# Scores in the four quarters of the array, and token group 0's product operands made during batch 1's attention

## The chip, the cores and the metric

The kernel runs on one core of one Trainium2 chip. The metric is the device time of one execution in microseconds (us). The engines are named as in the profile: PE is TensorE's matmul side, PEld its weight loads, DVE VectorE, ACT ScalarE, POOL GpSimd, SP the engine that issues the DMAs.

## The reference, cut to what matters

Attention with a window of 128 keys over 2 batches, 8 heads, 576 tokens of head size 64; its output (1152 tokens of 512) goes through 4 experts that are all used, then through a gated layer.

```python
scores = scale * q @ k.T                      # per batch and head, 576x576, head size 64
mask = (rel >= 0) & (rel < 128)               # rel = query position - key position
scores = where(mask, scores - slope[h] * abs(rel), -1e9)
attn = exp(scores - max); attn = attn / (sum(attn) + 1e-9)
x = (attn @ v) as 1152x512
for e in range(4):                            # w1: 512x1024, w2: 1024x512
    out += p[:, e] * (relu(x @ w1[e]) @ w2[e])
xn = out / rms(out) * g                       # then silu(xn @ w_gate) * (xn @ w_val) @ w_out
```

## The kernel before

**Attention.** Work goes by pairs of heads: 2 batches x 4 pairs, called pair 0 to 7 here. The 576 queries of a pair are nine tiles `t` of 64, and both heads stand in one tile: `qS` comes from the host filled up with zeros, so that its 128 rows hold head A's 64 dimensions and head B's, and its 128 columns head A's 64 queries (zeros in B's rows) and head B's. One 128x128 matmul (L311) of up to 192 key columns gives a tile's scores of both heads. Two tiles share a PSUM buffer `s`, and there are two such buffers. DVE adds the bias and takes the row's extreme (L312, the rows call it CUSTOM_DVE_ANT_0, the listings of order ISA), ACT takes the exponential with its sum (L316), POOL multiplies by the reciprocal (L326). The results stand in a score buffer `tt`, of which there are two, for pairs taken by turns. `values` then transposes them on PE (`pst`, L348), ACT and DVE copy these out as `pt` and `pe` (L333, L335), and PE multiplies by v: `po` and, for the last query tile, `pp` (L354), 64 output columns a head, the two heads in the two column halves of the array. ACT and DVE write the result as a high and a low part, `xh` and `xl` (L371, L372). `values` of a pair is emitted after the scores of the pair behind it. The order on each engine inside this part is that of the emitting code as the tile framework schedules it.

**Fillers.** Batch 0 is token group 0, batch 1 group 1. Unit 0, the first half of expert 0, needs no sums: `hidden` (`psa`, L207) for group 0 runs as a filler of the attention of batch 1, then `mixed` (`psb`, L221, four token tiles) after it.

**Behind the attention** the code is laid out by `Plan`: each engine's order is fixed by hand-set costs (Plan.START, RATE) and due times. First unit 0's `hidden` for group 1 (8 groups of 12 matmuls, L207), then its `out_plain` for token tiles 4 to 8 (L782). Units 1 to 7 use a product scheme with 7 products instead of 8 (`products`, L678, of 6 matmuls each, 42 a call); a unit makes four such calls: weight halves 0 and 1 for group 0, then both for group 1. It needs three token operands as they are and four made from sums: `token_sums` (for each group 14 DVE operations of 576 columns and 4 on ACT; `stage`, `th`, `tl`), and sums of the weights (`load_unit`, `raw` and `wb`). For unit 1 all of that, for both groups, is planned on DVE and ACT behind the attention. DVE also splits `wa`, `op` and folds PSUM results into `y` (L810, L812). On each engine the instructions stand in that order, so one that waits holds up those behind it.

Token operand 4 overwrites a quarter of group 0's own `xh`, `xl`; it can only be made when the fillers have read that.

Of the kernel before, what the change touches and what calls it, by code (L numbers as in the profile page):

```python
# [11 lines left out]
F32 = mybir.dt.float32  # L12
# [4 lines left out]
ALU = mybir.AluOpType  # L17
# [129 lines left out]
def tile_fused(ctx: ExitStack, tc: tile.TileContext, qS, kS, vS, probs, w1, w2, wgv, wo, g, out):  # L147
# [93 lines left out]
    y = ypool.tile([P, NTT, DM], F32, tag="y", name="y")  # L241


    h = hpool.tile([P, 4, NT], F32, tag="h", name="h")
    with (
# [15 lines left out]
        rel = rl_p.tile([P, WIN], F32, name="rel")  # L261
        bias = rl_p.tile([P, H // 2, WIN], F32, name="bias")
        for r in range(2):
# [14 lines left out]
        def load_pair(b, p):  # L278
            qt = qk_p.tile([P, NQ, P], F32, tag="q", name="qt")
            kt = qk_p.tile([P, S], F32, tag="k", name="kt")  # L280
            nc.sync.dma_start(out=kt, in_=kS[b, p])
            for t0, t1 in ((0, 3), (3, NQ)) if (b, p) == (0, 0) else ((0, NQ),):
                state["dma"] = nc.sync.dma_start(out=qt[:, t0:t1, :], in_=qS[b, p, :, t0:t1, :])
            if p % 2 == 0:
                vt = v_p.tile([P, 5, 4 * D], F32, tag="v", name="vt")
                hs = slice(p * P, p * P + 4 * D)
                nc.sync.dma_start(out=vt[:, :4, :], in_=vS[b, : 4 * P, hs].rearrange("(k p) d -> p k d", p=P))
                nc.sync.dma_start(out=vt[:D, 4, :], in_=vS[b, 4 * P :, hs])
                state["vt"] = vt
            if b == 0:  # L290
                for r in range(2):
                    rows = slice(r * D, (r + 1) * D)
                    nc.vector.tensor_scalar(
                        out=bias[rows, p, :], in0=rel[rows], scalar1=-8.0 * 2.0 ** (-8.0 * (2 * p + r + 1) / H), scalar2=None,
                        op0=ALU.mult,
                    )
            return qt, kt, state["vt"]

        def scores(n, p, qt, kt):
            tt = tts[n % 2]  # L300
            st = st_p.tile([P, 4, NQ], F32, tag="st", name="st")
            spans = []
            for t in range(NQ):
                k0 = max(0, t - 2) * D
                nk = (t + 1) * D - k0
                if t % 2 == 0 or t == NQ - 1:
                    s = ps_s.tile([P, 2, 4 * D], F32, tag="s", name="s")
                sp = s[:, t % 2, :nk]
                c0 = WIN - nk + (D if t % 2 else 0)
                spans.append(tt[:, t, c0 : c0 + nk])  # L310
                nc.tensor.matmul(sp, lhsT=qt[:, t, :], rhs=kt[:, k0 : k0 + nk], start=True, stop=True)  # L311
                nc.vector.tensor_tensor_reduce(  # L312
                    out=spans[t], in0=sp, in1=bias[:, p, WIN - nk :], scale=-0.125, scalar=3.0e38,
                    op0=ALU.add, op1=ALU.min, accum_out=st[:, 0, t : t + 1],
# [22 lines left out]
        def values(b, p, tt, vt):  # L337
            pt = pt_p.tile([P, 4, 4, P], F32, tag="pt", name="pt")
            pe = pt_p.tile([D, P], F32, tag="pe", name="pe")
            po = ps_o.tile([P, 4 * P], F32, tag="po", name="po")  # L340
            pp = ps_p.tile([P, D], F32, tag="pp", name="pp")
            for kb in range(5):
# [14 lines left out]

                for j in range(2):
                    r = slice(j * D, (j + 1) * D)
                    if kb < 4:  # L360
                        m = min(n, 4 if kb < 3 else 2)
                        mm(j, po[r, kb * P : kb * P + m * D], pt[:, kb, :m, r], kb == 0, kb == 3)
                for j in range(2):
                    r = slice(j * D, (j + 1) * D)
                    if kb == 3:
                        mm(j, pp[r, :], pt[:, 3, 2, r], True, False)
                    if kb == 4:
                        mm(j, pp[r, :], pe[:, r], False, True)
            for ps, w, o in ((po, 4 * P, 0), (pp, D, 4 * P)):
# [4 lines left out]
        def filler():  # L374
# [12 lines left out]
            for t in range(4):  # L387
                yield lambda t=t: mixed(t)

        state = {}  # L390
        order = [(b, p) for b in range(B) for p in range(H // 2)]
        ready, queue = [], []
        todo = filler()
        for n in range(len(order) + 1):
# [24 lines left out]


# [3 lines left out]
    tpool = ctx.enter_context(tc.tile_pool(name="tpool", bufs=1))  # L424
    HT = S // 2
    th = [xh] + [tpool.tile([P, 2, S], F32R, name=f"th{i}") for i in range(3)]
    tl = [xl] + [tpool.tile([P, 2, S], F32R, name=f"tl{i}") for i in range(3)]
    pl = Plan()
# [48 lines left out]
    class Stage:  # L477
# [6 lines left out]
        def first(self, engines, n, needs, emit, due):  # L484
            def emit_first(e):
                self.tile = tmp.tile([P, 512 if self.tag == "s" else S], F32, tag=self.tag, name="stage", bufs=RINGS[self.tag])
                emit(e)

            return pl.later(engines, n, needs, emit_first, due, (rings[self.tag], self.done))
# [3 lines left out]


    def second(n, gr):

        a, b = slice(gr * S, gr * S + HT), slice(gr * S + HT, (gr + 1) * S)
        k, tok = {0: (0, a), 1: (2, a), 2: (2, b), 4: (0, b)}.get(n, (0, slice(gr * HT, (gr + 1) * HT)))
        i = {3: 3, 5: 1, 6: 2}.get(n, 0)
        return [x[:, k : k + 2, tok] for x in (th[i], tl[i])]  # L500

    def operand(hi, lo, end):
        return (lambda k: hi[:, k, :]), (lambda k: lo[:, k, :]), end
# [555 lines left out]
```

## Time and profile before

| | |
|---|---|
| time, median of 3 runs | 696.7 us (696.02 to 697.32) |
| profiled execution: its time / its span | 696.54 / 694.8 us |
| busy in the span | PE 98%, PEld 88%, DVE 64%, ACT 42%, POOL 7% |
| attention (first scores to the last `psa`) | 4.8 to 82.8 us |
| unit 0's `psb` | 85.35 to 96.09 us |
| unit 0 for group 1, `hidden` and `out_plain` | 96.09 to 122.25 us |
| unit 1's four calls of `products` start at | 122.25, 128.13, 142.86, 148.44 us |

A busy PE is a matmul in flight, not PE at its peak. Stretches, waits and the chain are read by time, since the bound is not the same in each.

### The profile page before, as it was taken

What the parts mean: (1) busy time and instruction counts of PE and PEld (TensorE: products, weight loads), DVE (VectorE), ACT (ScalarE), POOL (GpSimd) and SP (SyncE); (2) the same over time, 40 slices, a digit from 0 to 9 for tenths busy, and PEclk for the clock granted to TensorE, in tenths of its full rate; (3) what the DMA queues carried; (4) which work ended last, traced back from release to release, by engine and by line L of the source; (5) the groups of instructions that cost most, each with busy time, mean ns of one, the idle gap of its engine ahead of it and who ended that gap; (6) DMA issues with size and microseconds to landing.
All of it is one profiled execution on the core that took longest, in us unless ns stands there. A gap on an engine that the chain in (4) does not pass through costs nothing.

```text
span 694.8 us, 10177 instructions
## 1 busy us (share of the span) xinstructions
PE 681.3 (98%) x3928; PEld 610.4 (88%) x3928; DVE 445.9 (64%) x946; ACT 295.0 (42%) x666; POOL 47.8 (7%) x100
## 2 busy tenths in 40 slices
PE   8999999699999999999999999999999999999997
PEld 6777798698998988989989989889998999899986
DVE  5765558868477585584784865887887775831233
ACT  5876533354262352442533524754546534411210
POOL 5852310000000000000000000000000000000000
PEclk9999999799999999999999999999999999999999
DMA  8650001112103002012030030103434441200012
GB/s 284 227 191 28 1 1 32 31 60 63 59 2 121 1 31 92 1 32 90 1 92 31 19 103 16 62 0 122 152 122 145 136 144 62 91 1 1 1 45 92
DMA packets 16304, 48.38 MB, mean 70 GB/s; under 512 B 1792, under 2 KB 4224, under 8 KB 16256
## 3 DMA queue, kind: packets, MB, share of 16 engines
q1 hardware_dynamic: 16256, 47.74, 20.8%
q8 instruction: 31, 0.51, 0.3%
q14 instruction: 17, 0.14, 0.1%
HBM read 45.37 MB, written 2.36 MB: 69 GB/s over the span
## 4 chain that ended last, share of the span: by engine, by line
PE 93%; DVE 4%; DMA 1%; ACT 1%; issue 0%; SPq 0%; POOL 0%; DVEq 0%
PE ps_b L782 11%; PE ps_d L782 9%; PE ps_a L782 9%; PE ps_c L782 8%; PE ps_c L678 7%; PE ps_b L207 6%; PE ps_d L678 6%; PE ps_c L207 6%; PE ps_d L207 5%; PE ps_a L207 5%; PE ps_a L678 5%; PE ps_b L678 4%; PE s L311 3%; PE po L354 3%; PE pst L348 2%; PE psa L207 2%
## 5 line engine op out<-in xcount | busy, mean ns | idle before, releaser
L782 PE MATMUL ps_b<-wa,op 128*128 128x512 f32 x348 | 82.2, 390 | 0.0
L782 PEld LDWEIGHTS ps_b<-wa,op 128*128 128x128 f32 x348 | 64.8, 188 | 13.0
L447 ACT ACTIVATE op<-h 128x512 fp32r<-128x512 f32 x95 | 56.5, 621 | 35.2 <-PE ps_d L782 11.9
L782 PE MATMUL ps_d<-wa,op 128*128 128x512 f32 x288 | 67.8, 390 | 0.0
L440 DVE TENSOR_TENSOR op<-h,op 128x512 fp32r<-128x512 f32 x95 | 63.0, 684 | 6.3 <-ACT op L447 6.0
L782 PEld LDWEIGHTS ps_d<-wa,op 128*128 128x128 f32 x288 | 54.0, 188 | 11.1
L782 PE MATMUL ps_a<-wa,op 128*128 128x512 f32 x264 | 61.8, 389 | 0.0
L782 PEld LDWEIGHTS ps_a<-wa,op 128*128 128x128 f32 x264 | 49.5, 188 | 10.2
L782 PE MATMUL ps_c<-wa,op 128*128 128x512 f32 x240 | 56.2, 389 | 0.0
L782 PEld LDWEIGHTS ps_c<-wa,op 128*128 128x128 f32 x240 | 45.1, 188 | 9.3
L207 PE MATMUL ps_b<-xh,wb 128*128 128x384 f32 x160 | 42.4, 335 | 0.0
L447 ACT ACTIVATE wb<-raw 128x512 fp32r<-128x512 f32 (+1 forms) x63 | 30.6, 526 | 22.6 <-DVE raw L440 22.6
L207 PE MATMUL ps_a<-xh,wb 128*128 128x384 f32 x144 | 38.3, 336 | 0.7 <-ACT xh L447 0.7
L739 ACT ACTIVATE h<-r 128x576 f32<-128x576 f32 x28 | 19.2, 686 | 46.6 <-DVE r L443 46.6
L207 PE MATMUL ps_c<-xh,wb 128*128 128x384 f32 x144 | 38.0, 334 | 0.0
L316 ACT ACTIVATE tt<-tt,st 128x192 f32<-128x192 f32 (+2 forms) x72 | 30.8, 429 | 11.0 <-DVE st L312 10.5
L440 DVE TENSOR_TENSOR wb<-raw,wb 128x512 fp32r<-128x512 f32 (+1 forms) x63 | 34.0, 567 | 0.5
L207 PE MATMUL ps_d<-xh,wb 128*128 128x384 f32 x128 | 33.9, 334 | 0.0
L608 ACT ACTIVATE stage<-raw 128x512 f32<-128x512 f32 x36 | 23.9, 666 | 21.8 <-DMA raw<-in_wo 12.1
L311 PE MATMUL s<-kt,qt 128*128 128x192 f32 (+1 forms) x144 | 31.7, 333 | 1.2 <-DMA qt<-in_qS 0.8
L312 DVE CUSTOM_DVE_ANT_0 tt<-s,bias 128x192 f32<-128x192 f32 (+2 forms) x72 | 23.3, 331 | 12.7 <-PE s L311 9.3
L326 POOL TENSOR_SCALAR tt<-tt,st 128x192 f32<-128x192 f32 (+2 forms) x72 | 27.9, 408 | 31.7 <-DVE st L324 15.7
(200 smaller groups left out, 1535.7 us busy)
## 6 DMA issues: line engine op xcount, KB each, us to landing
raw<-in_w SPq DMA_DIRECT2D x32, 512.0 KB, 3.6
raw<-in_wgv SPq DMA_DIRECT2D x24, 512.0 KB, 3.7
raw<-in_wo SPq DMA_DIRECT2D x12, 512.0 KB, 3.5
qt<-in_qS SPq DMA_DIRECT2D x7, 576.0 KB, 5.3
kt<-in_kS SPq DMA_DIRECT2D x8, 288.0 KB, 3.2
out_y<-acc SPq DMA_DIRECT2D x9, 256.0 KB, 2.0
vt<-in_vS SPq DMA_DIRECT2D x4, 512.0 KB, 5.1
qt<-in_qS SPq DMA_DIRECT2D x1, 384.0 KB, 4.5
```

Of the source, the lines that this page charges most:

```text
L207: nc.tensor.matmul(ps, lhsT=a, rhs=x[:, k, tok], start=(n == 0), stop=(n == 3 * KC - 1))
L311: nc.tensor.matmul(sp, lhsT=qt[:, t, :], rhs=kt[:, k0 : k0 + nk], start=True, stop=True)
L312: nc.vector.tensor_tensor_reduce(out=spans[t], in0=sp, in1=bias[:, p, WIN - nk :], scale=-0.125, scalar=3.0e38, op0=ALU.add, op1=ALU.min, ...
L316: nc.scalar.activation(out=spans[t], in_=spans[t], func=AF.Exp, bias=st[:, 0, t : t + 1], scale=-1.0, accum_out=st[:, 1, t : t + 1],)
L326: nc.gpsimd.tensor_scalar(out=spans[j], in0=spans[j], scalar1=st[:, 3, j : j + 1], scalar2=1.0, op0=ALU.mult, op1=ALU.mult,)
L354: nc.tensor.matmul(out, lhsT=vt[:nk, kb, v], rhs=rhs, start=start, stop=stop, skip_group_check=True,)
L440: EN[e].tensor_tensor(out=out, in0=a, in1=b, op=ALU.subtract)
L447: nc.scalar.activation(out=out, in_=a, func=AF.Copy)
L608: j = st.first("a", 512, [hr] + needs, lambda e: nc.scalar.activation(out=st.tile, in_=words(1, F32), func=AF.Copy, scale=2.0**-112,), due)
L678: nc.tensor.matmul(ps, lhsT=s[:, k, :], rhs=t(k), start=start and m == 0, stop=m == 5, skip_group_check=True,)
L739: return wrote(gr, pl.now("a", tok.stop - tok.start, needs + was_reading[gr], lambda e: nc.scalar.activation(out=h[:, c, tok], in_=src, fu ...
L782: nc.tensor.matmul(ps, lhsT=a(s)[:, k, :], rhs=w[k][0]()[:, i, :], start=(n == 0), stop=(n == 11))
```

## The change

- **Scores in quarters.** q comes without zeros, half as many bytes. A tile's scores are two matmuls of 64 rows and 64 columns, one a head, that take their rows of q and k from partition 0 or 64. For an even `t` head A's go to output partitions 0 to 63 and head B's to 64 to 127, for an odd one the other way round, so that the four matmuls of two tiles have the four quarters of the array. `bias` gets a second copy with the heads swapped, made on POOL (8 operations of 64x192).
- **Buffers.** `s` holds one tile and there are three of them; the bank for the third is that of `pp`, which moves into the `pst` buffer of the last key block, and its four matmuls stand together. `po`'s second operand picks its blocks by the parity of `t`.
- **A score buffer in y.** The second `tt` is columns of `y`, token tiles 4 to 8, which are written later.
- **Sums.** Group 0's operands are made by `sums()`: 12 of its 18 steps are emitted one behind each odd query tile of pairs 5 to 7 (in the order as built, their ten DVE operations stand within pairs 5 and 6), the last six (operands 4 and 3) with the `psb` tiles. `Plan` is left with group 1's. `th`, `tl` are split by group for that.

```diff
-        tc.tile_pool(name="ps_s", bufs=2, space=PSUM) as ps_s,
+        tc.tile_pool(name="ps_s", bufs=3, space=PSUM) as ps_s,
-        tc.tile_pool(name="ps_p", bufs=1, space=PSUM) as ps_p,
-        tts = [rl_p.tile([P, NQ, 4 * D], F32, name=f"tt{i}") for i in range(2)]
+        tts = [
+            rl_p.tile([P, NQ, 4 * D], F32, name="tt"),
+            y[:, 4:, :].rearrange("p a b -> p (a b)")[:, : NQ * 4 * D].rearrange("p (t c) -> p t c", t=NQ),
+        ]
-            qt = qk_p.tile([P, NQ, P], F32, tag="q", name="qt")
+            qt = qk_p.tile([P, S], F32, tag="q", name="qt")
-            for t0, t1 in ((0, 3), (3, NQ)) if (b, p) == (0, 0) else ((0, NQ),):
-                state["dma"] = nc.sync.dma_start(out=qt[:, t0:t1, :], in_=qS[b, p, :, t0:t1, :])
+            state["dma"] = nc.sync.dma_start(out=qt, in_=qS[b, p])
+                    for i, eng in enumerate((nc.vector, nc.gpsimd)):
+                        eng.tensor_scalar(
+                            out=bias[rows, p, i, :], in0=rel[rows], scalar1=-8.0 * 2.0 ** (-8.0 * (2 * p + (r ^ i) + 1) / H),
...
+            def pair(t0):
+                ts = range(t0, min(t0 + 2, NQ))
+                for t in ts:
+                    k0 = max(0, t - 2) * D
+                    nk = (t + 1) * D - k0
+                    sps.append(ps_s.tile([P, 4 * D], F32, tag="s", name="s")[:, :nk])
...
+                for t in ts:
+                    k0 = max(0, t - 2) * D
+                    for r in range(2):
+                        rows, o = slice(r * D, (r + 1) * D), (r ^ t & 1) * D
+                        nc.tensor.matmul(
+                            sps[t][o : o + D, :], lhsT=qt[rows, t * D : (t + 1) * D], rhs=kt[rows, k0 : (t + 1) * D],
+                            start=True, stop=True,
+                        )
             for t in range(NQ):
-                nc.tensor.matmul(sp, lhsT=qt[:, t, :], rhs=kt[:, k0 : k0 + nk], start=True, stop=True)
+                if t % 2 == 0:
+                    pair(t)
...
+                if t % 2:
+                    some(1)
...
-            pp = ps_p.tile([P, D], F32, tag="pp", name="pp")
+                    blocks = pt[:, kb, :m, :].rearrange("p (a b) (c d) -> p a (b c) d", b=2, c=2)
+                        mm(j, po[r, kb * P : kb * P + m * D], blocks[:, :, 1:3, :] if j else blocks[:, :, ::3, :], kb == 0, kb == 3)
+                    pp = pst[:, 2, :D]
...
+        def sums():
+            def keep(n, i):
+                hi, lo = second(n, 0)
+                yield lambda: nc.scalar.activation(out=hi, in_=st[i], func=AF.Copy)
+                yield tt(ALU.subtract, lo, st[i], hi.bitcast(F32))
+            yield tt(ALU.subtract, st[0], ch, dh)
+            yield tt(ALU.add, st[0], st[0], cl)
+            yield tt(ALU.subtract, st[0], st[0], dl)
+            yield from keep(6, 0)
...
+            yield from keep(5, 1)
+            yield None
+            yield from keep(4, 0)
+            yield tt(ALU.subtract, st[0], bh, st[1])
+            yield tt(ALU.add, st[0], st[0], bl)
+            yield from keep(3, 0)
+            if (b, p) == (1, 0):
+                steps = sums()
-        for f in todo:
+        for i, f in enumerate(todo):
             f()
+            if i >= 1:
+                some(3)
+        some(99)
...
-    first, k = token_sums(0, End(0.0), End(0.0), 8)
+    first = [operand(*second(n, 0), End(0.0)) for n in range(7)]
-    right = [first, token_sums(1, k, w1_read, 28)[0]]
+    right = [first, token_sums(1, End(0.0), w1_read, 28)[0]]
```

Three places show what moves.

PE, the values of pair 1 among the scores of pair 3, before (`s` scores, `pst` transposes, `po` and `pp` the products with v, `tt_119` and `tt_118` the score buffers of pairs 1 and 2):

```order
L311 MATMUL s<-kt,qt 128x128
L311 MATMUL s<-kt,qt 128x192
L354 MATMUL po<-pt,vt 64x256 x4
L354 MATMUL po<-pt,vt 64x128 x2
L354 MATMUL pp<-pt,vt 64x64 x2
L348 MATMUL pst<-ident,tt_119 64x128
L311 MATMUL s<-kt,qt 128x192 x2
L354 MATMUL pp<-pe,vt 64x64 x2
L348 MATMUL pst<-ident,tt_118 128x128
```

and with the change (`y` there is the score buffer of pair 1):

```order
L385 MATMUL po<-pt,vt 64x256 x2
L379 MATMUL pst<-ident,y 128x128 x4
L333 MATMUL s<-kt,qt 64x192 x3
L385 MATMUL po<-pt,vt 64x256 x4
L379 MATMUL pst<-ident,y 128x128 x3
L379 MATMUL pst<-ident,y 64x128
L333 MATMUL s<-kt,qt 64x192 x4
L385 MATMUL po<-pt,vt 64x128 x2
L402 MATMUL pst<-pt,vt 64x64 x2
L402 MATMUL pst<-pe,vt 64x64 x2
L333 MATMUL s<-kt,qt 64x192 x5
```

Scores stand in stretches of 2 to 20 quarter matmuls, some cut at an odd number, and now have a tile shape of their own between the transposes (128x128) and `po` (128x64).

DVE at the end of pair 6's scores, before (ISA is the bias step, `pt` and `pe` the copies out of the transposes, `xl` the low part):

```order
L335 COPY pt<-pst 128x512
L323 TENSOR_SCALAR st<-st 128x4
L324 RECIPROCAL st<-st 128x4
L335 COPY pe<-pst 64x128
L372 TENSOR_TENSOR xl<-po,xh 128x512
L372 TENSOR_TENSOR xl<-pp,xh 128x64
L312 ISA tt_119,st<-s,bias 128x64
```

and with the change:

```order
L433 TENSOR_TENSOR stage<-stage,xl 128x576
L342 ISA tt,st<-s,bias 128x192
L342 ISA st 128x1
L367 COPY pt<-pst 128x512
L355 TENSOR_SCALAR st<-st 128x4
L367 COPY pt<-pst 128x512
L356 RECIPROCAL st<-st 128x4
L433 TENSOR_TENSOR stage<-xh,stage 128x576
L433 TENSOR_TENSOR stage<-stage,xl 128x576
L367 COPY pe<-pst 64x128
L433 TENSOR_TENSOR tl_96<-stage,th_93 128x576
L409 TENSOR_TENSOR xl<-po,xh 128x512
```

Steps of group 0's sums (L433) now stand in DVE's queue ahead of copies and bias steps for which PE waits.

DVE from unit 0's last fold into `y` on, before (`x`, `r` are the results of unit 1's products; the first `x` belongs to its first call):

```order
L810 TENSOR_SCALAR y<-ps_b,pn_sb 128x512
L440 TENSOR_TENSOR raw<-raw 128x256
L440 TENSOR_TENSOR tl_1177<-stage,th_1174 128x2x288
L443 TENSOR_TENSOR x<-ps_b,x 128x288
L440 TENSOR_TENSOR stage<-xh 128x576
L443 TENSOR_TENSOR r<-ps_d,x 128x288
L443 TENSOR_TENSOR r<-ps_d,r 128x288
L443 TENSOR_TENSOR stage<-stage,xl 128x576
L440 TENSOR_TENSOR wb<-raw,wb 128x512
L440 TENSOR_TENSOR stage<-stage,xl 128x576
```

and with the change:

```order
L882 TENSOR_SCALAR y<-ps_b,pn_sb 128x512
L519 TENSOR_TENSOR raw<-raw 128x256
L519 TENSOR_TENSOR wa<-raw,wa 128x512
L522 TENSOR_TENSOR x<-ps_b,x 128x288
L519 TENSOR_TENSOR wb<-raw,wb 128x512
L522 TENSOR_TENSOR r<-ps_d,x 128x288
L522 TENSOR_TENSOR r<-ps_d,r 128x288
L519 TENSOR_TENSOR wa<-raw,wa 128x512
L522 TENSOR_TENSOR r<-ps_d,x 128x288
```

No sum of tokens stands behind unit 0's last fold any more, and the `wb` here is unit 1's last; before, two more `wb` and nine more operations on `stage`, `th`, `tl` and `raw` came behind the rows shown.

## Rows read from the trace of the kernel before

**Rows 1.** The page: the span, and busy time with its share and instructions.

```profile
span 694.8 us, 10177 instructions
PE 681.3 (98%) x3928; PEld 610.4 (88%) x3928; DVE 445.9 (64%) x946; ACT 295.0 (42%) x666; POOL 47.8 (7%) x100
```

**Rows 2.** Waits of PE, 0 to 200 us: waited for, us, times, longest.

```profile
PE ps_a L678 <- DVE wb L440: 3.7, 2, 2.0
PE ps_a L678 <- ACT wb L447: 1.6, 1, 1.6
PE s L311 <- DMA qt<-in_qS: 0.8, 2, 0.7
```

**Rows 3.** Busy time by stretch around unit 1's second and third call.

```profile
core 0: us, PE busy (x) PEld busy (x) DVE busy (x) ACT busy (x) POOL busy (x), PEclk, DMA share, GB/s
128.10:143.00 14.90, 9.63 (x46) 8.82 (x45) 11.14 (x20) 5.22 (x10) 0.00 (x0) 0.66 0.23 71
143.00:148.50 5.50, 5.50 (x44) 5.50 (x43) 4.68 (x9) 3.29 (x7) 0.00 (x0) 1.00 0.30 95
```

**Rows 4.** Timeline of PE there: start, us, form, count, idle before.

```profile
122.25 0.29 PE L678 MATMUL ps_b<-xh,wb 128*128 128x288 f32 x1
...
128.13 0.30 PE L678 MATMUL ps_a<-xh,wb 128*128 128x288 f32 x1
...
135.47 0.85 PE L678 MATMUL ps_a<-th,wb 128*128 128x288 f32 x2 [1.63 <-DVE wb L440]
...
142.86 0.29 PE L678 MATMUL ps_b<-xh,wb 128*128 128x288 f32 x1
...
148.44 0.29 PE L678 MATMUL ps_a<-xh,wb 128*128 128x288 f32 x1
```

**Rows 5.** Timeline of DVE there: a sum, and the last weights of unit 1.

```profile
132.72 0.76 DVE L440 TENSOR_TENSOR stage<-xh,stage 128x576 f32<-128x576 f32 x1
...
134.73 0.68 DVE L440 TENSOR_TENSOR wb<-raw,wb 128x512 fp32r<-128x512 f32 x1
```

**Rows 6.** DVE's operations on the stages alone (x), by stretch.

```profile
83.00:88.00 5.00, 4.36 (x3) 1.00 0.00 0
98.00:111.00 13.00, 8.17 (x11) 1.00 0.01 1
```

**Rows 7.** All of DVE (x), from the end of psb on.

```profile
96.10:128.10 32.00, 26.73 (x45) 1.00 0.05 17
96.10:135.40 39.30, 33.93 (x58) 0.95 0.04 14
```

**Rows 8.** The chain: PE pieces of the attention, start and us.

```profile
12.98 0.58 PE po L354 x2
13.55 0.85 PE s L311 x4
14.40 0.58 PE po L354 x4
...
40.65 1.01 PE po L354 x6
...
48.05 0.52 PE s L311 x2
```

**Rows 9.** The chain's DMA before pair 1's scores, and PE's timeline there.

```profile
3.81 6.33 DMA qt<-in_qS
...
10.27 0.41 PE L311 MATMUL s<-kt,qt 128*128 128x64 f32 x2 [0.66 <-DMA qt<-in_qS]
```

**Rows 10.** A stretch of the attention, as rows 3; a DVE sum under POOL, later.

```profile
50.00:60.00 10.00, 10.00 (x73) 7.49 (x72) 5.59 (x27) 6.87 (x24) 2.65 (x7) 1.00 0.27 90
...
84.05 1.86 DVE L443 TENSOR_TENSOR stage<-stage,xl 128x576 f32<-128x576 f32 x1
```

**Rows 11.** Timeline of PE: the first scores of pairs 5 and 7.

```profile
42.41 0.71 PE L311 MATMUL s<-kt,qt 128*128 128x64 f32 x4
...
64.94 0.71 PE L311 MATMUL s<-kt,qt 128*128 128x64 f32 x4
```

More of the change, by code (lines that the diff above doesn't have):

```diff
@@ L1 @@
+import itertools
 import math
@@ L241, in tile_fused, with second @@
     y = ypool.tile([P, NTT, DM], F32, tag="y", name="y")
+    HT = S // 2
+    tpre = ctx.enter_context(tc.tile_pool(name="tpre", bufs=1))
+    th = [xh] + [[tpre.tile([P, 2, HT], F32R, name=f"th{i}"), None] for i in range(3)]
+    tl = [xl] + [[tpre.tile([P, 2, HT], F32R, name=f"tl{i}"), None] for i in range(3)]
+    def second(n, gr):
+        a, b = slice(gr * S, gr * S + HT), slice(gr * S + HT, (gr + 1) * S)
+        k, tok = {0: (0, a), 1: (2, a), 2: (2, b), 4: (0, b)}.get(n, (0, None))
+        i = {3: 3, 5: 1, 6: 2}.get(n, 0)
+        return [x[:, k : k + 2, tok] if i == 0 else x[gr] for x in (th[i], tl[i])]
     h = hpool.tile([P, 4, NT], F32, tag="h", name="h")
@@ L261, in tile_fused @@
         rel = rl_p.tile([P, WIN], F32, name="rel")
-        bias = rl_p.tile([P, H // 2, WIN], F32, name="bias")
+        bias = rl_p.tile([P, H // 2, 2, WIN], F32, name="bias")
         for r in range(2):
@@ L292, in load_pair @@
                     rows = slice(r * D, (r + 1) * D)
[L293 to L296, printed above, removed]
+                    for i, eng in enumerate((nc.vector, nc.gpsimd)):
+                        eng.tensor_scalar(
+                            out=bias[rows, p, i, :], in0=rel[rows], scalar1=-8.0 * 2.0 ** (-8.0 * (2 * p + (r ^ i) + 1) / H),
+                            scalar2=1.0, op0=ALU.mult, op1=ALU.mult,
+                        )
             return qt, kt, state["vt"]
@@ L388, in filler, with tt, some @@
                 yield lambda t=t: mixed(t)
+        def sums():
+            st = [tpre.tile([P, S], F32, tag="t", name="stage", bufs=RINGS["t"]).rearrange("p (a b) -> p a b", a=2) for _ in range(2)]
+            (ah, al), (bh, bl), (ch, cl), (dh, dl) = ([x.bitcast(F32) for x in second(n, 0)] for n in (0, 1, 2, 4))
+            def tt(op, out, a, b):
+                return lambda: nc.vector.tensor_tensor(out=out, in0=a, in1=b, op=op)
+            def keep(n, i):
[6 more added lines that the diff above has]
+            yield from keep(6, 0)
+            yield tt(ALU.subtract, st[0], dh, ah)
+            yield tt(ALU.add, st[0], st[0], dl)
+            yield tt(ALU.subtract, st[0], st[0], al)
+            yield tt(ALU.subtract, st[1], ch, st[0])
+            yield tt(ALU.add, st[1], st[1], cl)
+            yield from keep(5, 1)
[4 more added lines that the diff above has]
+            yield from keep(3, 0)
+        def some(n):
+            for f in itertools.islice(steps, n):
+                if f is None:
+                    return
+                f()
         state = {}
@@ L392, in tile_fused @@
         ready, queue = [], []
+        steps = iter(())
         todo = filler()
@@ L424, in tile_fused @@
     tpool = ctx.enter_context(tc.tile_pool(name="tpool", bufs=1))
-    HT = S // 2
-    th = [xh] + [tpool.tile([P, 2, S], F32R, name=f"th{i}") for i in range(3)]
-    tl = [xl] + [tpool.tile([P, 2, S], F32R, name=f"tl{i}") for i in range(3)]
+    made = []
+    for x in th[1:] + tl[1:]:
+        x[1] = tpool.tile([P, 2, HT], F32R, name="t1", tag=f"t1_{len(made)}")
+        made.append(x[1])
     pl = Plan()
@@ L485, in emit_first @@
             def emit_first(e):
-                self.tile = tmp.tile([P, 512 if self.tag == "s" else S], F32, tag=self.tag, name="stage", bufs=RINGS[self.tag])
+                self.tile = (tpre if self.tag == "t" else tmp).tile([P, 512 if self.tag == "s" else S], F32, tag=self.tag, name="stage", bufs=RINGS[self.tag])
                 emit(e)
@@ L492, in cols @@
             return self.tile[:, a:b]
[L495 to L500, printed above, removed]
     def operand(hi, lo, end):
```

45 lines of the change are left out of this document (21 added, 24 removed).

## The prediction

> **What bounds the kernel now.** First the page: PE has a matmul in flight for 681.3 of 694.8 us [rows 1], so the change can gain in two ways only: where PE stands still or slow, and where PE's own work gets shorter. Then PE's waits up to 200 us: 5.3 us for DVE and ACT to deliver `wb`, weights of unit 1, and 0.8 us for q [rows 2]. Then the stretches around those waits: from 128.1 to 143.0 us PE is busy for 9.63 us of 14.90, at a mean granted clock of 0.66, where the stretch behind it has PE busy throughout at 1.00 for nearly as many matmuls, 44 against 46 [rows 3]. Two levels, 1.2 and 2.4 GHz, mix there: the clock fell after PE had stood in gaps of 1.6 us and more. The timeline gives the price: the second call of `products` lasts from 128.13 to 142.86 us, 14.73 us, the third, of the same 42 matmuls, 5.58 us (142.86 to 148.44), the first 5.88 (122.25 to 128.13) [rows 4]. So one hole costs 9.15 us in the second call and 0.3 in the first: **9.45 us**, of which the waits are little more than half.
>
> Why it is there: DVE is late. PE wants the weights at 128.13 and runs on at 135.47 us, when DVE's last `wb` of unit 1, begun at 134.73, is there; among DVE's last steps ahead of it are sums of tokens, as the one at 132.72 [rows 4, 5]. From the end of `psb` to that point DVE works for 33.93 of 39.30 us [rows 7]. It is the bound of this stretch, not a chain of waits.
>
> In the attention PE is in flight all the time (10.00 of 10.00), DVE at 56%, ACT at 69%, POOL at 27% from 50 to 60 us [rows 10]. PE bounds it.
>
> **The change part by part.**
>
> *Sums, behind the attention.* The 14 DVE operations of group 0's sums lie at 83 to 88 (3) and at 98 to 111 us (11, 8.17 us) [rows 6]. The eleven go from the stretch in which DVE is late. By the order, DVE has 56 operations between its last `y` of `psb` and unit 1's last `wb` before the change, and 40 with it (3 of group 1's sums have also slipped ahead, among the `psb` tiles). At the durations in the trace (0.76 us for 576 columns, 0.68 for 512 [rows 5], and in the same proportion for the rest) that is 36.1 us before, measured as 33.9 since they overlap a little, and 25.1 now. PE needs 32.0 us for its own work from that point until it wants those weights (96.1 to 128.13). So DVE is some 7 us early where it was 7.3 us late (135.47 less 128.13). What is late next? The first `wa` of unit 1, wanted two calls later; the same DVE time pays for that. The waits of DVE inside the stretch were 5.3 us before (32.00 less 26.73 [rows 7]) and fit into the 7. The hole goes, with its slow clock, since nothing else in it made PE stand. **-9.45 us**; if a third of it stayed, -6.3.
>
> *Sums, inside the attention.* Ten DVE operations now stand within pairs 5 and 6, 22.5 us long before (first scores of pair 5 at 42.41, of pair 7 at 64.94 us [rows 11]). DVE's 56% [rows 10] are 12.6 us of these; ten sums of 0.76 us make it 20.2, which fits but is tight. One such sum, run beside a POOL instruction, took 1.86 us instead of 0.76 [rows 10]; if all ten did, DVE would need 31.2 us in 22.5, and PE would wait. POOL is busy for 27% of the time here. On DVE's queue the bias steps, that free the score buffers, and the copies `pt` and `pe` stand behind them, and PE waits for both; the fillers `psa` cover part of that. Bounds 0 and +8.7; I take **+0.7**, near the lower end, since POOL is idle most of the time. Four of the six later steps are DVE's and lie beside `psb`, at 86 to 97 us, where DVE waits for PE.
>
> *Scores, the stream.* Two score matmuls in a row take 0.85 us, one alone 0.52, so a tile of 192 keys streams for 0.33 us, and 0.19 is the cost of changing the tile shape of the array and back into it [rows 8]. Before, eight pairs of 64+128+7x192 columns make 64 such steps: 21.1 us. With four quarters at a time the order's 30 stretches of quarter matmuls hold 46 groups of up to four, worth 41.7 full steps by width: 13.8 us. That quarters run at once no row shows; the nearest are the column halves of `po`: one matmul takes 0.58 us, two side by side 0.58 too, and a further step 0.43 (1.01 less 0.58) [rows 8]. Halves overlap fully, so I take it for quarters: **-7.3 us**. From the other side, without any overlap, twice as many matmuls of the same length: +21.1.
>
> *Scores, the changes of shape.* By the order the attention has 66 changes of tile shape before and 99 now, since the scores no longer share the transposes' shape. `po` alone takes 0.58 for a stream of 0.43: 0.15 us a change, for a shape with short weight loads as the quarters have [rows 8]. 33 more: **+5.0 us**, between 0 and 6.3 (at 0.19).
>
> *q at half the size.* Pair 1's scores begin at 10.27 us after PE stood 0.66 us for a q whose DMA took 6.33 us [rows 9]; both waits for q are 0.8 us [rows 2]. 288 KB less ahead of each: **-0.8 us**, at most -2 with pair 0's shorter steps. The eight new bias operations on POOL lie before its first scaling step and wait for nothing; pair 0's second tile may start 0.3 us later.
>
> *Buffers.* Three tiles instead of two pairs of tiles: a pair's second tile waits until DVE has read the one before it, and then its two quarters run by themselves. `pp` in the `pst` buffer holds that buffer until ACT and DVE have copied it, two steps longer. Neither has a row; each is covered while PE has transposes and fillers in between, and is at most a DVE bias step, 0.4 us, a tile pair. Taken at 0, up to +4. The score buffer in `y` is written by unit 0 long after its last reader: 0.
>
> *Sum.* -9.45 + 0.7 - 7.3 + 5.0 - 0.8 = -11.85 us. The profiled execution took 696.54 us (span 694.8), 0.2 under the median, so it stands for the runs: 696.54 - 11.85 = 684.7; I say **684.5 us**. Behind unit 1 the orders are the same and PE has no slack there that would eat the gain.
>
> **The rivals.**
>
> *The two row halves can't write one bank at once.* The scores of the two heads of one tile come from different row halves of the array and go to one PSUM buffer. Then the two take turns, each beside a matmul of the other tile at best: a pair of tiles takes 0.66 us as now, the stream gains nothing, the changes of shape stay: -9.45 + 0.7 + 5.0 - 0.8 = -4.5, **692 us**. Against it speaks `po`, whose two halves write one buffer at once [rows 8], but these are column halves. The Trainium skill states this rule (TensorEngine Tiling (Array Packing), Restrictions and Gotchas, PSUM Pressure: different row tiles cannot access the same PSUM bank simultaneously), while TensorE: Matmul & The Clock Gate, Part 3, tells of packings in rows and columns that ran at once; no run here shows row halves yet. By the first page the time would be this rival's, by the second the forecast.
>
> *Quarters don't overlap at all.* All 144 score matmuls then run one by one: +21.1 + 5.0 + 0.7 - 0.8 - 9.45 = +16.5, **713 us**. This is the slower side, one mechanism in the attention: it decides once the score stream grows by more than 4.5 us, that is when four quarters take longer than 1.9 steps (25.6 us over 41.7 steps of 0.33). The column halves speak against it.
>
> *DVE becomes the bound of pairs 5 and 6.* Sums at 1.4 us, halfway to the slow row, and PE waiting for the copies behind them: +4 to +5 in place of +0.7, **688.5 us**. For it: the tight 20.2 of 22.5 us.
>
> *The hole stays in part.* PE arrives 2 to 3 us earlier, ACT's steps between DVE's hold the `wb` up, a gap of some 2 us remains and brings the low clock again, as it did: half of the 9.45 is lost, **689.5 us**. Against it: 7 us in hand.
>
> **How the numbers follow.** Forecast 0.60 (own range 680 to 688), one bank 0.10, no overlap 0.07, DVE-bound 0.12, part of the hole 0.08, and 0.03 for losses in the buffers that eat all. Low end 680: changes of shape at a third of the price and a quicker start. High end 692 takes in both milder rivals and the bank; left out are the serial quarters, the rest, and a tail below 680, under 0.2. A difference of 0.2% (1.4 us) is about what a measurement of this kernel can tell from none. Faster 0.88, same 0.03, slower 0.09.
>
> **What would show it.** In the changed profile: the second call of `products` at 5.6 to 6 us and a granted clock of 1.00 all through; no wait of PE for `wb`. Four score matmuls starting within some 20 ns of each other, and pieces of `s` in the chain no longer than one step plus a change; if their starts lie 0.16 us or more apart, it is a rival's. The attention's end (last `psa`, now at 82.8 us) at 79 to 82; later than 83 means that buffers or DVE took the gain of the quarters. Sums of 576 columns at 1.4 us or more within pairs 5 and 6 would show the third rival. The forecast is wrong if the hole has a second cause that comes to light when DVE is early.

## The result, and the profile after

The changed kernel takes **687.09 us** (median, 686.73 to 687.25) against 696.36 of the kernel before beside it (695.76 to 697.32): ratio 0.9866, 95% interval 0.9853 to 0.9879. The forecast was 684.5 us, in a range of 680 to 692. The sign and the main term came as forecast, the gain was 9.3 us instead of 11.85. A part of the agreement is luck: several terms were wrong, with opposite signs.

The page of the changed kernel; its first lines answer to [rows 1]. Its last line is the granted clock of TensorE in 40 slices of the span, in tenths:

```profile
span 685.4 us, 10489 instructions
...
PE 674.2 (98%) x4072; PEld 595.7 (87%) x4072; DVE 443.4 (65%) x946; ACT 293.1 (43%) x666; POOL 54.2 (8%) x108
...
PEclk9999999999999999999999999999999999999999
```

The same line of the kernel before has a dip in its eighth slice, at unit 1's second call, and now there is none:

```profile
PEclk9999999799999999999999999999999999999999
```

PE's waits from 0 to 200 us, against [rows 2]. The waits for `wb` and for q are gone; the longest is new, in `psb`, for a copy of `y` on DVE:

```profile
PE psb L222 <- DVE y L419: 1.4, 1, 1.4
...
PE po L385 <- DVE pt L367: 1.1, 1, 1.1
PE s L333 <- DVE st L342: 0.7, 2, 0.5
```

The stretches of unit 1's first three calls of `products`, against [rows 3, 4]: 5.9, 5.6 and 5.6 us, PE busy throughout, clock 1.00.

```profile
121.60:127.50 5.90, 5.84 (x43) 5.57 (x43) 4.17 (x8) 1.38 (x3) 0.00 (x0) 1.00 0.21 78
127.50:133.10 5.60, 5.60 (x44) 5.60 (x43) 3.49 (x7) 2.77 (x6) 0.00 (x0) 1.00 0.34 108
133.10:138.70 5.60, 5.60 (x45) 5.60 (x44) 4.05 (x8) 3.29 (x7) 0.00 (x0) 1.00 0.29 94
```

The calls' starts on PE's timeline give the hole's price to two decimals: 14.73 us before, 133.10 less 127.53, that is 5.57, now. **-9.16 us**.

```profile
121.64 0.29 PE L750 MATMUL ps_b<-xh,wb 128*128 128x288 f32 x1
...
127.53 0.30 PE L750 MATMUL ps_a<-xh,wb 128*128 128x288 f32 x1
...
133.10 0.30 PE L750 MATMUL ps_b<-xh,wb 128*128 128x288 f32 x1
...
138.68 0.30 PE L750 MATMUL ps_a<-xh,wb 128*128 128x288 f32 x1
```

Where the rest went is read from first starts on PE's timeline, for the two kernels and for the experiments told below (us; "before" is the profile of [rows 1 to 11]):

| kernel | time | ratio to before (95%) | first score | pair 2's scores | `psb` | group 1's `hidden` |
|---|---|---|---|---|---|---|
| before | 696.36 | | 4.76 | 17.16 | 84.26 | 95.93 |
| after | 687.09 | 0.9866 (0.9853-0.9879) | 4.89 | 13.74 | 81.93 | 95.32 |
| quarters_only | 694.42 | 0.9974 (0.9964-0.9984) | 4.90 | 13.87 | 82.53 | 94.19 |
| sums_only | 685.87 | 0.9851 (0.9838-0.9864) | 5.12 | 15.38 | 80.33 | 93.73 |
| rest_only | 694.03 | 0.9966 (0.9954-0.9978) | 5.79 | 16.83 | 82.74 | 94.40 |
| sums_old | 687.94 | 0.9877 (0.9862-0.9892) | 5.21 | 17.70 | 83.09 | 96.49 |
| sums_pp | 690.83 | 0.9922 (0.9906-0.9939) | 5.11 | 18.88 | 85.76 | 99.15 |
| two_buffers | 691.81 | 0.9933 (0.9920-0.9945) | 4.89 | 17.08 | 86.68 | 100.10 |
| halves | 690.42 | 0.9918 (0.9905-0.9932) | 4.90 | 13.87 | 85.23 | 98.64 |
| parts_dve | 684.90 | 0.9837 (0.9824-0.9851) | 4.90 | 13.74 | 81.92 | 92.94 |
| best | 685.08 | 0.9835 (0.9820-0.9850) | 5.85 | 16.78 | 81.77 | 92.79 |
| best_split | 683.76 | 0.9824 (0.9811-0.9838) | 4.54 | 16.13 | 80.96 | 91.97 |
| hybrid | 683.69 | 0.9819 (0.9806-0.9833) | 4.90 | 15.33 | 80.80 | 91.83 |

Before against after: the attention ends 2.33 us earlier (`psb` at 81.93), `psb` then lasts 13.39 us instead of 11.67 and gives back 1.72, from there to the first call of `products` it is 26.32 us in both, the first call lasts 5.9 in both, the second is the 9.16, and from the third call's start to the end 0.35 us is lost (546.33 to 546.68), which no run takes apart. -2.33 + 1.72 - 9.16 + 0.35 = -9.4, the difference of the spans. The starts here are those of the first record of each kind. In the kernel before, the last `psa` starts at 84.12 us and `psb` at 84.26; the table ahead of the prediction has 82.8 and 85.35 for them, which are not the last record of the one and the first of the other.

### The profile page after: what moved, and what is told of

The parts are those of the page before. It is cut to its first block, busy times and chain, and to the rows that moved or that the text cites. A ratio compares the mean times of both kernels' runs of the same rounds, so it can differ in the third digit from the quotient of the medians.

```text
span 685.4 us, 10489 instructions
## 1 busy us (share of the span) xinstructions
PE 674.2 (98%) x4072; PEld 595.7 (87%) x4072; DVE 443.4 (65%) x946; ACT 293.1 (43%) x666; POOL 54.2 (8%) x108
## 4 chain that ended last, share of the span: by engine, by line
PE 94%; DVE 4%; ACT 1%; issue 0%; POOL 0%; POOLq 0%; DVEq 0%
PE ps_b L854 12%; PE ps_d L854 10%; PE ps_a L854 9%; PE ps_c L854 8%; PE ps_c L750 7%; PE ps_d L750 7%; PE ps_b L208 6%; PE ps_c L208 6%; PE ps_d L208 5%; PE ps_a L208 5%; PE ps_a L750 5%; PE ps_b L750 4%; PE s L333 3%; PE pst L379 3%; PE po L385 2%; PE psa L208 2%
## 5 line engine op out<-in xcount | busy, mean ns | idle before, releaser
L519 DVE TENSOR_TENSOR op<-h,op 128x512 fp32r<-128x512 f32 x95 | 63.1, 684 | 7.2 <-ACT op L526 6.8
L519 DVE TENSOR_TENSOR wb<-raw,wb 128x512 fp32r<-128x512 f32 (+1 forms) x63 | 34.1, 566 | 1.4 <-ACT wb L526 0.8
L208 PEld LDWEIGHTS ps_b<-xh,wb 128*128 128x128 f32 x160 | 29.1, 188 | 0.1
L526 ACT ACTIVATE wa<-raw 128x512 fp32r<-128x512 f32 x28 | 16.1, 621 | 28.2 <-DMA raw<-in_w 28.2
L208 PE MATMUL ps_b<-xl,wb 128*128 128x384 f32 x80 | 26.8, 336 | 0.3 <-DVE xl L519 0.3
L750 PE MATMUL ps_c<-xh,wb 128*128 128x288 f32 x112 | 27.0, 297 | 0.0
```

What stands on the lines that cost most here:

```text
L208: nc.tensor.matmul(ps, lhsT=a, rhs=x[:, k, tok], start=(n == 0), stop=(n == 3 * KC - 1))
L519: EN[e].tensor_tensor(out=out, in0=a, in1=b, op=ALU.subtract)
L526: nc.scalar.activation(out=out, in_=a, func=AF.Copy)
L750: nc.tensor.matmul(ps, lhsT=s[:, k, :], rhs=t(k), start=start and m == 0, stop=m == 5, skip_group_check=True,)
```

## The experiments

**One part at a time.** `quarters_only` takes the moved sums back:

```
-            if (b, p) == (1, 0):
-                steps = sums()
-    first = [operand(*second(n, 0), End(0.0)) for n in range(7)]
+    first, k = token_sums(0, End(0.0), End(0.0), 8)
```

> The changed kernel with one part undone: group 0's sums are made behind the attention again, in the planner's order, as in the kernel before; the quarter scores, three score buffers and the half-size q stay. Theory (the change's gain is the hole, 9.2 us, plus a small gain in the attention of which about 1.7 us is given back in psb): the hole is back, the second product call of unit 1 takes 14 to 15 us at a granted clock well below 1.00, the attention ends 2.5 to 3.5 us earlier than before (psb starts at 81 to 82 us instead of 84.26), and psb keeps that gain because no sum stands ahead of its first y copy, so some 693 to 694 us. Rival (the hole was gone already because PE and DVE are spaced differently, or the quarters carry most of the gain): 687 to 689 us with no wait for wb.

694.42 us. The hole is back where it was, as the stretch of the second call shows (14.6 us, clock 0.65):

```profile
126.40:141.00 14.60, 9.41 (x44) 8.52 (x43) 11.04 (x20) 5.22 (x10) 0.00 (x0) 0.65 0.20 73
```

The theory holds in the main: moving the sums is worth 7.3 us net (694.42 to 687.09), and `psb` lasts 11.66 us again, without the wait for `y`. The gain in the attention is smaller than expected: `psb` starts at 82.53 us, 1.73 earlier than before, where 2.5 to 3.5 had been named.

`sums_only` takes the quarters back instead:

```
-                    for r in range(2):
-                        nc.tensor.matmul(sps[t][o : o + D, :], lhsT=qt[rows, t * D : ...], rhs=kt[rows, ...])
+                    nc.tensor.matmul(sps[t], lhsT=qt[:, t, :], rhs=kt[:, k0 : (t + 1) * D], ...)
```

> The changed kernel with the other part undone: scores over the full array again, with the zero-padded q of full size, one score tile per buffer and one bias copy; the sums in the attention and in psb stay as changed. Theory (hole worth 9.2 to 9.45 us, sums in the attention cost 0 to 0.7 us, quarters gain 2 to 3 us): no wait for wb, second product call 5.6 us, psb starts 84.3 to 85.5 us, and psb loses the same 1 to 2 us as in the changed kernel; about 688.5 to 690 us. Rival (sums cost the attention much, and the quarters hide it): psb starts at 87 us or later and the time is above 691 us. Rival (quarters gain nothing): 687 us.

685.87 us: faster than the changed kernel, and below every expectation. `psb` starts at 80.33 us, 1.6 earlier than with quarters. So the quarters cost 1.2 us. The 95% intervals of the two ratios overlap, since the runs of the kernel before scatter by 1.5 us, but the runs themselves don't (685.56 to 685.99 against 686.73 to 687.25), and `parts_dve` against `best_split` below says 1.1 once more. And yet with full-array scores `psb` starts 3.9 us earlier than before. The quarters can't have done that; the sums or the buffers must have, and the next runs part them.

`rest_only` has neither (the edits of both runs together); what stays is the three score buffers of one tile each, scores issued two tiles at a time, and `pp` in the transposes' buffer.

> Neither the quarters nor the moved sums: full-array scores, group 0's sums behind the attention; what is left of the change is the third score buffer with one tile in each, the scores issued two tiles at a time, and pp in the buffer of the transposes. Theory (these buffers and the order that follows from them shorten the attention by about 4 us, since all halves of po then stand side by side in PE's order and scores wait less; the quarters and the sums have no part in it): psb starts at 80 to 81 us, the hole of about 9 us is there, 692 to 693 us. Rival (the attention got shorter by the moved sums or by a better start): psb starts at 83 to 84.5 us, 695 to 696.5 us.

694.03 us, 2.3 under before, with the hole. It lies between the theory (692 to 693) and the rival (695 to 696.5). The first score came at 5.79 us, 0.7 later than in `sums_only`, after a wait of 0.8 us for the full-size q; but `psb` at 82.74 is also later than the 80 to 81 expected by more than that. From the first score to `psb` it is 76.95 us against 79.50 before: the buffers do shorten the attention, but by 2.55 us and not by all of the 3.9.

`sums_old` and `sums_pp` split that. `sums_old` has the moved sums in the attention of the kernel before (two score buffers of two tiles, `pp` in its own; the first q comes in one load, and one `tt` stays in `y`); `sums_pp` also has `pp` in the transposes' buffer:

```
-                        mm(j, pp[r, :], pt[:, 3, 2, r], True, False)
-                        mm(j, pp[r, :], pe[:, r], False, True)
+                    pp = pst[:, 2, :D]      # four matmuls at the end, behind pe
```

> The moved sums alone, with the attention of the kernel before: two score buffers of two tiles each, pp in a buffer of its own, full-array scores. Theory (the sums cost the attention 0 to 1 us and remove the hole, 9.2 us; psb loses 1 to 2 us to them): psb starts at 84 to 85.3 us, no wait for wb, 688 to 689.5 us. Rival (the moved sums themselves reorder PE and shorten the attention): psb starts below 83 us, 686 to 687 us.

> The run with the moved sums alone, and one thing more: pp lies in the buffer of the transposes, with its four matmuls at the end, as in the changed kernel; the two score buffers of two tiles each and full-array scores stay as in the kernel before. Theory (the third score buffer, not the place of pp, is what shortens the attention by 2 us): as with the sums alone or a little slower, since the order has 72 changes of tile shape instead of 65 and as many lone halves of po: 687.7 to 689 us, psb starts at 83 to 84.3 us. Rival (pp's four matmuls in a row are the gain): 685.8 to 686.3 us, as with the sums and all the buffers changed.

687.94 and 690.83 us. `sums_old` ended between its theory and its rival. From pair 2's scores to `psb` it takes 65.39 us against 67.10 before: up to pair 5's scores the two are alike (25.27 and 25.25 us), and the 1.7 us are gained behind them, where the sums stand. So the moved sums shorten the attention by themselves, and are a part of `sums_only`'s 3.9; how stays open. `pp`'s new place costs 2.9 us by itself, more than either theory had it; its rival is refuted with it. The runs of `sums_pp` scatter more than the others (689.10 to 693.21), so this price and the next are good to some 2 us. The step from there to `sums_only` brings 5.0 (690.83 to 685.87). It isn't the third buffer alone: three buffers of one tile take the place of two of two, and scores are issued two tiles at a time. `two_buffers` takes the third buffer alone away, from the changed kernel:

```
-        tc.tile_pool(name="ps_s", bufs=3, space=PSUM) as ps_s,
+        tc.tile_pool(name="ps_s", bufs=2, space=PSUM) as ps_s,
```

> The changed kernel with two score buffers instead of three; everything else, the quarters and the sums too, stays. By the order PE then has 126 changes of tile shape instead of 98 or 99 and more halves of po that stand alone. Theory (PE bounds the attention and a change of shape costs 0.16 us, a lone half 0.43): 27 x 0.16 + 3 x 0.43 = 5.6 us more at most, less where the waits between scores shrink in turn: psb starts at 85.5 to 87.5 us, 690.5 to 692.5 us. Rival (the third buffer is of no weight because DVE and ACT set the pace of the scores): psb starts at 82 to 83 us, 687 to 688 us.

691.81 us, 4.7 more, as the theory says. So the parts in a row are: sums -8.4, `pp` +2.9, score buffers -5.0, quarters with the half-size q +1.2; together -9.3. In another order they have other sizes: taken away last, the sums are worth 7.3.

**Why the quarters don't pay.** They do run at once: in the changed kernel's records the four quarters of two tiles start 6 to 7 ns apart (66.401, 66.407, 66.414, 66.421 us). A score matmul stands in the records as two passes. The chain has pieces of twelve passes (six quarter matmuls, the scores of three tiles) in 0.80 us, where four full passes (two matmuls, two tiles) took 0.85 [rows 8]:

```profile
65.89 0.58 PE po L385 x2
66.47 0.80 PE s L333 x12
67.27 0.58 PE po L385 x2
```

But they seldom come in fours. Counting passes that start within 25 ns as a group, the 288 score passes stand in 125 groups: 24 of four, 12 of three, 67 of two, 22 alone. A pair of tiles needs two free buffers of three, and DVE frees one at a time. Of the 32 pairs of tiles, 9 start with all four quarters at once; in 19 of the other 23, DVE's bias step that frees the second tile's buffer ended only after the first tile had started (in pair 0, tiles 4 and 5, those steps end at 6.308 and 6.517 us, and the quarters start at 6.372 and 6.581). In the last four both buffers were free, and PE's order put other work between. From the records, each pass's start to the next group's start, split into the stream (0.160 us for a pass of 192 columns, in proportion for others; 0.12 for a filler's), and what goes beyond it where the tile shape changes and where it doesn't, from the first score to `psb` (us):

| | before | after | sums_only | sums_pp | two_buffers | halves |
|---|---|---|---|---|---|---|
| stream of the scores | 20.48 | 17.81 | 20.48 | 20.48 | 16.27 | 25.01 |
| stream of transposes, `po`, `pp` | 29.87 | 27.73 | 27.31 | 29.01 | 29.01 | 27.73 |
| stream of the fillers | 11.52 | 11.52 | 11.52 | 11.52 | 11.52 | 11.52 |
| beyond it, at changes of shape (number) | 6.36 (66) | 11.62 (98) | 6.46 (66) | 7.27 (72) | 14.39 (125) | 9.91 (98) |
| beyond it, elsewhere (waits too) | 11.27 | 8.34 | 9.44 | 12.36 | 10.60 | 6.16 |
| sum | 79.50 | 77.02 | 75.21 | 80.64 | 81.79 | 80.33 |

The quarters save 2.67 us of stream and pay 5.26 for 32 more changes of shape (1.1 of it is the wait of `po` for `pt`). The Trainium skill says that changing the tiling mode drains TensorE (TensorEngine Tiling (Array Packing), Key Properties); the table agrees and gives the price, about 0.1 us each (6.36 over 66, 10.5 over 98 without that wait, 14.39 over 125) and 0.13 for each of the 32 that are new. `two_buffers` makes it plain: more of its pairs of tiles start together (15 of 32) and its scores have the shortest stream of all, but its 125 changes are the dearest, and it is the slowest but for those with the hole.

The second row is a gain that nobody had asked for. Before, six pairs of `po`'s two column halves stood apart in PE's order and streamed one after the other (rows of two passes, 0.65 us, each half by itself); in `sums_only` all 32 pairs stand side by side, eight passes in 1.08 us, and in the changed kernel 31. Before:

```profile
15.18 0.65 PE L311 MATMUL s<-kt,qt 128*128 128x192 f32 x3
15.76 0.65 PE L354 MATMUL po<-pt,vt 128*64 128x256 f32 x2
16.34 0.33 PE L348 MATMUL pst<-ident,tt 128*128 128x128 f32 x1
```

and in `sums_only`:

```profile
24.24 1.14 PE L327 MATMUL s<-kt,qt 128*128 128x192 f32 x6
25.22 0.41 PE L388 MATMUL pst<-ident,y 128*128 128x128 f32 x2
25.56 1.08 PE L394 MATMUL po<-pt,vt 128*64 128x256 f32 x8
```

Six lone halves at 0.427 us are 2.56 us: `sums_only`'s 27.31 against 29.87.

`halves` keeps matmuls, sizes and changes of shape, but doesn't swap the odd tiles, so that only two quarters can work at once:

```
-                        rows, o = slice(r * D, (r + 1) * D), (r ^ t & 1) * D
+                        rows, o = slice(r * D, (r + 1) * D), r * D
```

> The changed kernel with the odd score tiles no longer swapped: head 0 always goes from rows 0-63 to columns 0-63 and head 1 from rows 64-127 to columns 64-127, so only two of the four quarters can work at once; the count of matmuls and of changes of tile shape (99) is the same. Theory (a pair of tiles then streams for 0.66 us instead of 0.33 and PE bounds the attention): the stream grows by about 7 us, psb starts at 88 to 89 us, 693 to 694.5 us. Rival (within pairs DVE's bias steps and the score buffers bound the scores, the quarters are ahead of them anyway): 687 to 690 us, with psb starting at 82 to 85 us.

690.42 us, `psb` at 85.23 (+3.3): between the two. The stream of the scores does grow by the theory's 7 us (17.81 to 25.01, with 173 groups instead of 125), but half of it comes back: 1.7 us at the changes of shape and 2.2 elsewhere, as the table has it. Up to pair 2 nothing is lost at all (13.87 us against 13.74): in pairs 0 and 1, which have no fillers, DVE, ACT and the buffers pace the scores, not PE.

**What `psb` gives back.** In the changed kernel four DVE sums (three of group 0's, L433, and one of group 1's, L519) stand ahead of the first copy `y <- psb`, and take 1.4 to 1.85 us each, where later ones take 0.74. DVE's timeline, and under it POOL's and PE's:

```profile
82.21 1.38 DVE L433 TENSOR_TENSOR xl<-stage,xh 128x576 fp32r<-128x576 f32 x1 [1.52 <-ACT xh L437]
83.62 1.74 DVE L433 TENSOR_TENSOR stage<-xh,stage 128x576 f32<-128x576 f32 x1
85.39 1.74 DVE L433 TENSOR_TENSOR stage<-stage,xl 128x576 f32<-128x576 f32 x1
87.06 1.85 DVE L519 TENSOR_TENSOR stage<-xh 128x576 f32<-128x576 f32 x1
88.83 0.74 DVE L419 TENSOR_SCALAR y<-psb,pn_sb 128x512 f32<-128x512 f32 x1
89.49 0.74 DVE L433 TENSOR_TENSOR tl<-stage,th 128x576 fp32r<-128x576 f32 x1
```

```profile
81.69 6.59 POOL L179 TENSOR_TENSOR op<-h,op 128x512 fp32r<-128x512 f32 x4 [9.84 <-ACT op L178]
```

```profile
83.03 5.27 PE L222 MATMUL psb<-wa,op 128*128 128x512 f32 x22 [0.47 <-POOL op L179]
89.71 5.77 PE L222 MATMUL psb<-wa,op 128*128 128x512 f32 x24 [1.42 <-DVE y L419]
```

`psb` has two buffers, so its third token tile waits for the first copy. `parts_dve` moves POOL's four subtractions to DVE:

```
-                a = token_parts(op_p.tile([P, 2, 512], F32R, tag="oa", name="op"), t, "ap")
+                a = token_parts(op_p.tile([P, 2, 512], F32R, tag="oa", name="op"), t, "ad")
```

> The changed kernel with one engine moved: the low parts of the tokens that are made at the end of the attention run on DVE instead of POOL, so POOL is idle while DVE makes the last sums. Theory (the sums beside psb take 1.4 to 1.85 us because POOL's long tensor_tensor runs at the same time, and that delays the y copy that frees psb's buffer): the 576-column sums of DVE after 82 us take about 0.76 us, PE's wait for the copy of y (1.4 us) goes, and the first product call of group 1 starts 1.2 to 1.7 us earlier relative to psb's start; 685 to 686 us. Rival (the sums take 1.4 us for another reason, such as their operands, or the low parts now on DVE cost as much as POOL's contention did): the wait stays at 1 us or more and the time is 686.5 to 688.5 us.

684.90 us. With four operations more on it, DVE is ready sooner: the sums take 0.75 us, the copy stands at 85.45, both waits of `psb` are gone, and it lasts 11.02 us instead of 13.39.

```profile
83.51 0.75 DVE L433 TENSOR_TENSOR stage<-xh,stage 128x576 f32<-128x576 f32 x1
84.18 0.68 DVE L179 TENSOR_TENSOR op<-h,op 128x512 fp32r<-128x512 f32 x1
84.78 0.75 DVE L433 TENSOR_TENSOR stage<-stage,xl 128x576 f32<-128x576 f32 x1
85.45 0.74 DVE L419 TENSOR_SCALAR y<-psb,pn_sb 128x512 f32<-128x512 f32 x1
```

```profile
81.92 11.18 PE L222 MATMUL psb<-wa,op 128*128 128x512 f32 x48
```

**Both together.** `best` is `sums_only` with `parts_dve`'s edit; `best_split` also loads the first q in two parts, as the kernel before did; `hybrid` uses the quarters and the half-size q in pairs 0 and 1 only, where PE is not the bound.

> Two parts of the changed kernel altered together: full-array scores with the zero-padded q as in the run with the sums alone, and the low parts at the end of the attention on DVE instead of POOL. Theory (the two gains, 1.2 us in the attention and 2.2 us in psb, stand in different stretches and add up): psb starts at 80.3 us and lasts 11.2 us, 683.5 to 684 us, faster than both kernels. Rival (one of the two gains only moved a wait that the other would pay as well): 684.7 to 686 us.

> Full-array scores in all pairs with low parts on DVE, and the first q load cut in two as in the kernel before. Theory (the lead of the quarters in pairs 0 and 1 is q's size, not the matmuls): the first score starts at 4.8 us, pair 1's scores still wait for q, pair 2 starts at 15 to 16.5 us, psb at 80 to 81.3 us, 683.3 to 684.6 us. Rival (the late start of 0.7 to 1 us was all that stood between the two): pair 2 starts at 14 us, 682 us.

> Quarters with the half-size q only in batch 0's pairs 0 and 1; full-array scores with the zero-padded q in the six pairs behind them; low parts at the end of the attention on DVE. Theory (the quarters help only where PE has no filler work and q is late, and their changes of shape cost more than they stream off behind that): pair 2 starts at 13.7 to 14 us as in the changed kernel, from there to psb 65 to 65.3 us as with full-array scores, psb starts at 78.7 to 79.3 us, 681.5 to 682.3 us. Rival (what is gained in pairs 0 and 1 is waited for later, at a q that is not there or at DVE): psb starts at 80 us or later, 683 us or more. Rival (quarters help in all pairs): slower than the changed kernel with the low parts on DVE, over 684.9 us.

`best` took 685.08 us, in the rival's range, but for another cause: pair 2 to `psb` is 64.99 us (64.95 in `sums_only`) and `psb` lasts 11.02, so that both gains are there; the first score was at 5.85 us, 0.73 later than in `sums_only`, and pair 1 waited 0.9 us for its q. `best_split` starts at 4.54 and takes **683.76 us**, as expected. `hybrid` takes 683.69, the same, in the range of its first rival (683 us or more): it has pair 2 at 15.33 instead of the 13.7 to 14 expected, since PE's order has `po` and transposes ahead of it (from 14.25 us), and from there needs 65.47 us. So a quarter of the array helps nowhere enough to be measured. Open in `best_split` are PE's two waits for q ahead of pair 2, which `hybrid` doesn't have:

```profile
PE s L328 <- DMA qt<-in_qS: 2.8, 2, 1.7
```

Both versions beat the kernel before by 1.8% and the changed one by 0.5%.

## Why the prediction was right, and where it was wrong

- **Hole, -9.45: right** (-9.16). The 0.3 us of the first call was not part of it, as that call still lasts 5.9. The margin came about as worked out, 7 us less some 5 of waits: the last `wb` for the second call begins at 124.19 us and takes 0.68, PE wants it at 127.53, so DVE is 2.7 us early; from the end of `psb` to there it is busy for 23.51 of 29.40 us, as its row among the stretches shows (against [rows 7]; behind the span stand busy us, count, clock and DMA):

```profile
95.50:124.90 29.40, 23.51 (x42) 1.00 0.06 19
```

- **Sums inside the attention, +0.7: the bound was wrong.** They cost nothing that shows: with them the way from pair 2's scores to `psb` is 0.96 us shorter with full-array scores (64.95 against `rest_only`'s 65.91) and 0.47 with quarters. DVE has room, the order around them moves too (66 changes of shape instead of 70), and POOL slows them little here (nine of the ten take 0.72 to 0.76 us, one 0.86). The low end should have been under nothing. The rival with DVE as the bound falls.
- **Stream, -7.3: the step that failed most.** That "the order's 30 stretches of quarter matmuls hold 46 groups" takes every stretch as packed four by four. The trace has some 62 groups for each of the two passes, and -2.67 us: most pairs of tiles start in twos, the second when DVE has freed its buffer. The overlap itself was right, which refutes the rivals of one bank and of no overlap. The Trainium skill's rule that row tiles can't access one PSUM bank at once (TensorEngine Tiling (Array Packing), Restrictions and Gotchas, PSUM Pressure) does not hold here: the two quarters of one tile lie in different row halves, write one buffer, and start 6 to 7 ns apart. They write different partitions of it; quarters that write the same ones were not tried. What the Trainium skill tells in TensorE: Matmul & The Clock Gate, Part 3, of packings in rows and columns that ran at once agrees with these starts.
- **Changes of shape, +5.0: right in size** (+5.26, or some 4.2 without the wait of 1.1 in it; 32 counted, 0.13 us each instead of 0.15).
- **q at half the size, -0.8: right** as far as its waits go; pair 1's scores start at 8.84 us instead of 10.27.
- **Buffers, 0 up to +4: the size taken was wrong, and so was the bound.** `pp`'s place costs 2.9 us, within the bound; the score buffers bring 5.0, and a gain was not weighed at all. Part of it is the lone halves of `po`: [rows 8] has one (12.98 us, two passes in 0.58), and it was read only as a sign that halves overlap.
- **The six later steps, 0: wrong, +1.7.** The prediction had the row in hand (1.86 us for a sum under POOL, [rows 10]) and used it only for pairs 5 and 6. Three of the four that "lie beside `psb`" lie beside POOL's subtractions too, and with a slowed sum of group 1 behind them they stand ahead of the first copy that frees PE's buffer.

In sum the attention's terms came to -2.4, measured -2.33, by errors that cancel: stream 4.6 worse, sums 1.2 better or more, buffers and lone halves 2 to 4 better. The sign set for the attention's end (79 to 82 us) started from 82.8; from 84.26 the same terms give 81.9, which is where `psb` starts. What the forecast missed in the total is `psb`'s 1.72 and some tenths behind it.

## What to carry to other kernels

Price a packing of the array by the groups that buffers and order let start together and by the changes of shape that it adds, not by the count of matmuls: here four quarters do run at once and still lose 1.2 us. Work that fits into an engine's idle share must be checked at both its new places for what stands behind it on that queue, and for a second engine that slows it there. An edit with several parts is worth taking apart: here one part (the sums) made nearly all of the gain, and two of the others cost time.

## What the runs showed of the hardware

DVE's two-input operations and POOL's operations hold each other up, and who pays was not the same beside two instructions of POOL. Under POOL's TENSOR_TENSOR a DVE sum takes 1.74 us instead of 0.75, and POOL's four take 6.59 us; without DVE's sums, in `quarters_only`, they take 5.02:

```profile
82.28 5.02 POOL L179 TENSOR_TENSOR op<-h,op 128x512 fp32r<-128x512 f32 x4 [11.21 <-ACT op L178]
```

Beside POOL's short TENSOR_SCALAR the sum nearly always keeps its time, and POOL pays: four of 192 columns take 2.20 us with a sum beside the first, five take 2.02 with none. POOL's timeline in the changed kernel, and DVE's there:

```profile
50.68 2.20 POOL L358 TENSOR_SCALAR y<-y,st 128x192 f32<-128x192 f32 x4 [0.61 <-DVE st L356]
...
69.82 2.02 POOL L358 TENSOR_SCALAR y<-y,st 128x192 f32<-128x192 f32 x5
```

```profile
50.63 0.76 DVE L433 TENSOR_TENSOR tl<-stage,th 128x576 fp32r<-128x576 f32 x1
```

The Trainium skill states the rule (SBUF — State Buffer, Who interferes with whom): a DVE instruction with two SBUF inputs contends with a GpSimd instruction that reads SBUF. The rows agree: 1.74 us instead of 0.75 on DVE, 6.59 instead of 5.02 on POOL. Whether the kind of POOL's instruction, its length or the order of the two starts decides who waits is not shown: beside the short one DVE's sum began 0.05 us ahead (50.63 against 50.68 us).
